# Different start addresses for the seven slots of the sequence batches

## The chip, the cores and the metric

The kernel runs on one core of one Trainium2 chip. The metric is the device time of one execution in microseconds (us). Before the change it is 725.52 us, the median of three runs (725.23 to 725.96).

## The reference, cut to what matters

```python
x = A_x                                             # 2048 x 576, float32
g = sigmoid((x * gate_w).sum(-1, keepdims=True))
a = linear_attention(x, A_wqkv, A_wo)               # 32 heads of 18
b = fourier(x)
out = g * a + (1 - g) * b

def fourier(x):
    a = einsum("bsd,ed->bse", x, dft_hid_re)        # 576 x 576
    b = einsum("bsd,ed->bse", x, dft_hid_im)
    return einsum("ts,bse->bte", dft_seq_re, a) - einsum("ts,bse->bte", dft_seq_im, b)
```

The change lies in the last line of `fourier`: two products of a 2048 x 2048 matrix with a 2048 x 576 matrix. The rest of the program (attention, and the products with the hidden-dimension matrices) are computed as before.

## The kernel before

**Precision.** TensorE multiplies in fp32r. Each float32 operand is split into a high part (ScalarE rounds a copy, helper `hi_of`, line 175) and a low part (VectorE subtracts, `lo_of`, line 185). A product takes three matmuls: high x low, high x high, low x high.

**Stages.** The keys and their features come first (lines 532 and 205), then the sums of keys and values (line 696), the queries and the output projection (line 205 again). Then come two pairs of stages: `Hidden.run` (line 979) makes the product of x with the real hidden matrix and leaves it on the chip as seven right-hand sides per pair of row blocks, after a scheme of the Strassen kind with seven products in place of eight. `sequence` (line 1133) multiplies the real sequence matrix with them. After that the same two stages run for the imaginary parts. The order of PE, ScalarE, VectorE and SyncE instructions is written out by hand.

**The right-hand sides** ("factors", tiles `fh` and `fl`) lie at `T_AT + p * TPAIR` for p = 0 to 7, seven rows of high and seven of low parts, each row 288 elements or 1152 bytes. `TPAIR` is 16128 bytes.

**The batches.** `sequence` runs over 32 batches: 8 row groups j by 4 batches b. One batch is 7 forms of 2 blocks of 128 x 128 of the sequence matrix, 7168 bytes in each partition (the constant `SLOT`). `Matrix.load` fetches four of the seven forms from HBM by one DMA of 512 KB on SyncE's queue (line 1070). `Matrix.make` forms the other three with VectorE (line 195), rounds all seven into a second tile, the high part (ScalarE, line 175), and subtracts in place, which leaves the low part (VectorE, line 185). In each of the 32 steps of `sequence` batch n + 3 is loaded, batch n + 2 is made, and batch n is multiplied: 7 products x 2 blocks x 3 matmuls = 42 matmuls, each with its own weight load of 128 x 128 from the batch and 288 columns of a factor.

**Where batches lie.** Seven slots of 7168 bytes lie one behind the other from `SLOT_AT`. Slots 3, 1, 4, 6 take the raw and later the low part of batch 1, 2, 3, 4 and so on in turn. Slots 2, 5, 0 take the high parts in turn. So twelve batches pass before a pair of slots comes again. Batch 0 lies elsewhere (`self.first`). 512 bytes lie between the end of the seventh slot and `Y_AT`; no batch uses them.

**What else uses this space.** `Hidden.run` keeps left-hand tiles (`xs`, `rests`) and weights (`w`) in the slots before batches need them. In the second `Hidden.run` (`swap` is 1) three groups of weights, `w(4)` to `w(6)`, lie from the start of slot 5 on, 4608 bytes each. They are loaded from HBM in the last steps of the first `sequence` (steps 28 and 29).

Of the kernel before, what the change touches and what calls it, by code (L numbers as in the profile page):

```python
# [20 lines left out]
HALF = D // 2  # L21
# [32 lines left out]
class Ring:  # L54


    def __init__(self, start, size, n):
        self.at, self.n = [start + i * size for i in range(n)], 0
# [11 lines left out]
SLOT_AT, SLOT = ACC_AT + NT * D * 4 + 256, 7 * BS * P * 4  # L70
# [21 lines left out]
class Layout:  # L92
# [5 lines left out]
    def __init__(self, swap):  # L98
        self.swap = swap
        slot = [SLOT_AT + k * SLOT for k in range(7)]  # L100
        self.low, self.high = [slot[k] for k in (3, 1, 4, 6)], [slot[k] for k in (2, 5, 0)]
        pair = [T_AT + p * TPAIR for p in range(NP)]
        self.first = pair[6], pair[7]
        self.xs = pair[1:6] if swap else [slot[0], slot[2], pair[4], pair[7], pair[5]]
        self.xs += [slot[0], slot[2], slot[0]]
        far, near = WF_AT + 4 * WF, slot[4]
        self.sums = pair[7] + SLOT + XR
        if swap:
            self.rests = [far, MIX_AT, pair[6] + SLOT, pair[6] + SLOT + XR, near, far,
                          pair[7] + SLOT, MIX_AT]  # L110
        else:
            self.rests = [near, MIX_AT, T_AT + 60416, MIX_AT + XR, far, near, MIX_AT, MIX_AT + XR]
# [10 lines left out]
    def w(self, k):  # L123
        if not self.swap:
            k = (0, 1, 2, 4, 5, 6, 3)[k]
        elif k > 3:
            return (SLOT_AT + 5 * SLOT + (6 - k) * 4 * HALF * 4,
                    (CONST_AT + 3584, CONST_AT + 3584 + HALF * 4, WF_AT + 4 * WF + XR)[k - 4])
        o = WF_AT + k * WF if k < 4 else SLOT_AT + 14 * XF + XR + (6 - k) * WF
        return o, o + 4 * HALF * 4  # L130
# [3 lines left out]
def kernel(  # L134
# [804 lines left out]
    class Hidden:  # L939
# [34 lines left out]
        def product(self, ps, p, k, start):  # L974
            x, (w, wl) = self.x[p, k], self.w[k]
            ops = [(x[:, a, c * P:c * P + P], w[:, 2 * c + b]) for c in range(2) for a, b in TURN]
            ops.append((self.rest[p][:96, 6 - k], wl[:96]))
            for n, (a, b) in enumerate(ops):
                nc.tensor.matmul(ps, a, b, start=(start and n == 0), stop=(n == len(ops) - 1),  # L979
                                 skip_group_check=True)  # L980
# [297 lines left out]
def _layouts(inputs):  # L1278
# [27 lines left out]
    def right(w):  # L1306

        main, rest = halves(w)
        quarters = ((0, 0), (1, 0), (1, 1), (0, 1))
        cols = (slice(0, HALF), slice(HALF, D))  # L1310
        main = np.stack([main[d][:, :, cols[c]] for d, c in quarters], axis=2)
        rest = np.stack([rest[d][:, cols[c]] for d, c in quarters], axis=1)
        return main, np.concatenate([rest] * 3)
# [42 lines left out]
```

## Time and profile before

| | |
|---|---|
| Median of the runs | 725.52 us |
| The profiled execution, its own time | 725.31 us |
| Its span, first to last instruction | 723.6 us |
| TensorE clock granted | 1.000 |
| PE busy | 718.9 us (99%) |
| VectorE (DVE) busy | 594.6 us (82%) |
| ScalarE (ACT) busy | 331.8 us (46%) |
| Line 1133 on the chain that ended last | 49% |

PE busy is the time in which a matmul was in flight; matmuls overlap, so PE is busy even where it runs below its best pace. The pace is better read as the number of matmuls that start in a stretch. The chain of work that ended last is followed back from the last instruction; its pieces, listed in order of time, show the stages one behind the other. A view of windows gives the busy time of each engine in chosen stretches. "Mean ns of one" of a matmul (about 294) is from its start to the modelled end of its results, more than twice the distance between two starts.

### The profile page before, as it was taken

The numbers are of one execution on the slowest core, as the hardware profiler recorded it, in microseconds if no ns is written. First come the engines' busy times: TensorE is split into PE (matmuls) and PEld (weight loads), VectorE is DVE, ScalarE is ACT, GpSimd is POOL, SyncE is SP. The second block draws the span as 40 slices with busy tenths as digits, with TensorE's granted clock in tenths as the row PEclk, the third lists the DMA queues.
The fourth block names the chain that finished last, engine by engine and source line by source line (L and its number), as shares of the span: only waits on it lengthen the run. The fifth ranks groups of instructions, "written<-read, shape, count | busy, mean of one in ns | idle before, by whom it ended". The sixth has DMA issues, their size and how long they took to land.

```text
span 723.6 us, 13786 instructions
## 1 busy us (share of the span) xinstructions
PE 718.9 (99%) x5436; PEld 718.3 (99%) x5436; DVE 594.6 (82%) x954; ACT 331.8 (46%) x519; POOL 54.1 (7%) x94
## 2 busy tenths in 40 slices
PE   9999999999999999999999999999999999999998
PEld 9999999999999999999999999999999999999997
DVE  5699876787999828989999999857889988778884
ACT  5998445678644534453434334223535432342331
POOL 1112200050131100000010000000000000000000
PEclk9999999999999999999999999999999999999999
DMA  7388887874594699544475586889963543454440
GB/s 256 105 286 297 305 304 214 295 223 118 182 358 177 228 321 388 160 153 131 157 249 189 167 289 198 287 313 401 380 214 130 175 143 136 125 179 153 153 154 34
DMA packets 54836, 157.83 MB, mean 218 GB/s; under 512 B 6388, under 2 KB 12084, under 8 KB 53748
## 3 DMA queue, kind: packets, MB, share of 16 engines
q1 hardware_dynamic: 45716, 118.44, 48.5%
q0 software_dynamic: 8768, 38.12, 14.5%
q8 instruction: 43, 0.70, 0.4%
q10 hardware_dynamic: 288, 0.39, 0.2%
q14 instruction: 21, 0.17, 0.1%
HBM read 114.06 MB, written 41.39 MB: 215 GB/s over the span
## 4 chain that ended last, share of the span: by engine, by line
PE 93%; DVE 6%; issue 0%; ACT 0%; DVEq 0%; POOL 0%; POOLq 0%
PE bank L1133 49%; PE bank L205 18%; PE bank L979 14%; PE bank L696 8%; PE bank L532 2%; DVE qs L185 1%; DVE acc L775 1%; DVE pz L767 1%; DVE den L768 1%; PE bank L231 1%; PE bank L678 0%; DVE xb L185 0%; DVE den L772 0%; PE bank L797 0%; DVE xb L195 0%
## 5 line engine op out<-in xcount | busy, mean ns | idle before, releaser
L1133 PE MATMUL bank<-fh,c 128*128 128x288 f32 x1792 | 354.7, 294 | 0.0
L1133 PEld LDWEIGHTS bank<-fh,c 128*128 128x128 f32 x1792 | 286.7, 188 | 0.0
L1133 PE MATMUL bank<-fl,c 128*128 128x288 f32 x896 | 263.6, 294 | 0.0
L175 ACT ACTIVATE c<-craw 128x1792 fp32r<-128x1792 f32 (+1 forms) x84 | 121.3, 1447 | 169.9 <-DVE craw L195 161.2
L1133 PEld LDWEIGHTS bank<-fl,c 128*128 128x128 f32 x896 | 168.7, 188 | 0.0
L185 DVE TENSOR_TENSOR c<-craw,c 128x1792 fp32r<-128x1792 f32 (+4 forms) x86 | 141.9, 1653 | 1.5 <-ACT c L175 1.4
L195 DVE TENSOR_TENSOR craw<-craw 128x256 f32<-128x256 f32 (+1 forms) x192 | 97.9, 512 | 22.0 <-DMA craw<-in_ci_dram 13.6
L205 PE MATMUL bank<-wd,xs 128*128 128x288 f32 (+1 forms) x784 | 105.9, 295 | 0.0
L205 PEld LDWEIGHTS bank<-wd,xs 128*128 128x128 f32 x784 | 104.6, 188 | 0.0
L979 PE MATMUL bank<-wf,xf 128*128 128x288 f32 x588 | 91.1, 295 | 0.0
L979 PEld LDWEIGHTS bank<-wf,xf 128*128 128x128 f32 x588 | 83.4, 189 | 0.0
L205 PE MATMUL bank<-mw,qs 128*128 128x288 f32 x448 | 61.8, 296 | 0.1
L696 PE MATMUL bank<-pk,c 128*128 128x288 f32 x448 | 60.6, 296 | 0.0
L205 PEld LDWEIGHTS bank<-mw,qs 128*128 128x128 f32 x448 | 59.8, 188 | 0.5 <-DVE qs L185 0.4
L696 PEld LDWEIGHTS bank<-pk,c 128*128 128x128 f32 x448 | 59.7, 189 | 0.0
L370 DVE SCALAR_TENSOR_TENSOR acc<-bank,e 128x288 f32<-128x288 f32 x64 | 28.5, 452 | 17.3 <-ACT e L369 17.1
L195 DVE TENSOR_TENSOR ys<-bank,ys 128x288 f32<-128x288 f32 x63 | 28.8, 456 | 16.0 <-PE bank L1133 12.6
L185 DVE TENSOR_TENSOR fl<-fl,fh 128x864 fp32r<-128x864 f32 (+1 forms) x32 | 34.5, 1093 | 6.6 <-ACT fh L175 5.3
L175 ACT ACTIVATE fh<-fl 128x864 fp32r<-128x864 f32 (+1 forms) x32 | 29.8, 950 | 16.6 <-DVE fl L195 16.6
L195 DVE TENSOR_TENSOR fl<-bank,y 128x288 f32<-128x288 f32 x48 | 21.6, 450 | 15.8 <-PE bank L979 15.8
L979 PE MATMUL bank<-wf,xr 96*128 96x288 f32 x112 | 33.3, 298 | 0.0
L195 DVE TENSOR_TENSOR ys<-ys,bank 128x288 f32<-128x288 f32 x47 | 21.2, 450 | 12.4 <-PE bank L1133 11.8
(106 smaller groups left out, 639.6 us busy)
## 6 DMA issues: line engine op xcount, KB each, us to landing
xf<-xm SPq DMA_DIRECT2D x42, 512.0 KB, 8.4
craw<-in_cr_dram SPq DMA_DIRECT2D x32, 512.0 KB, 3.6
craw<-in_ci_dram SPq DMA_DIRECT2D x32, 512.0 KB, 3.7
xm<-xb POOLq DMA_DIRECT2D x8, 1024.0 KB, 5.8
wf<-wm SPq DMA_DIRECT2D x14, 576.0 KB, 6.2
xraw<-in_xa_dram SPq DMA_DIRECT2D x25, 320.0 KB, 3.5
xr<-xr SPq DMA_DIRECT2D x14, 448.0 KB, 8.0
xm<-xb POOLq DMA_DIRECT2D x8, 768.0 KB, 7.4
```

What stands on the lines that cost most here:

```text
L175: return nc.scalar.activation(dst, src, AF.Copy, bias=bias)
L185: nc.vector.tensor_tensor(out=dst, in0=src, in1=hi, op=ALU.subtract)
L195: nc.vector.tensor_tensor(out=dst, in0=a, in1=b, op=op)
L205: nc.tensor.matmul(ps, a, b, start=(n == 0), stop=(n == len(pairs) - 1))
L231: nc.tensor.matmul(warm[:, :P], ones_f, ones_f, start=True, stop=True)
L370: nc.vector.scalar_tensor_tensor(dst, ps, 0.0, e, op0=ALU.max, op1=ALU.add)
L532: nc.tensor.matmul(ps[i][h], x[:, i_x * P:(i_x + 1) * P], wkt.row(h, j), start=(c == 0 and n == 0), stop=(c == KC and n == 1))
L696: nc.tensor.matmul(ps[h][:, :HALF], t[:, a, k], pk[s][:, b, half(h)], start=(s == 0 and n == 0), stop=(s == NT - 1 and n == len(passes) - 1))
L767: nc.vector.scalar_tensor_tensor(pz, acc[2 * k + i], EPS, zb, op0=ALU.add, op1=ALU.mult)
L768: nc.vector.tensor_reduce(out=d[:, i], in_=pz.rearrange("p (h d) -> p h d", d=DH), op=ALU.add, axis=AX.X)
L979: nc.tensor.matmul(ps, a, b, start=(start and n == 0), stop=(n == len(ops) - 1), skip_group_check=True)
L1133: nc.tensor.matmul(ps[q], c[x][:, l, k], factors[p](y, f), start=(p == 0 and i == 0), stop=(p == NP - 1 and i == 2))
```

## The change

The start of each slot's tile moves by an offset that is a multiple of 64 bytes. In the order in which they take turns, the slots for low parts move by 256, 64, 384 and 448 bytes, those for high parts by 64, 384 and 0. Modulo 256 bytes the low parts then start at 0, 64, 128, 192, and the high parts at 64, 128, 0. Before, all start at 0 (all of this relative to a base that all tiles share). No two slots overlap, and the last one stays inside the 512 bytes ahead of `Y_AT`. Weights `w(4)` to `w(6)` of the second `Hidden.run` move by 384 bytes, with slot 5. No instruction is added, removed or moved in its order.

```diff
     def __init__(self, swap):
         self.swap = swap
         slot = [SLOT_AT + k * SLOT for k in range(7)]
-        self.low, self.high = [slot[k] for k in (3, 1, 4, 6)], [slot[k] for k in (2, 5, 0)]
+        self.low = [slot[k] + o for k, o in ((3, 256), (1, 64), (4, 384), (6, 448))]
+        self.high = [slot[k] + o for k, o in ((2, 64), (5, 384), (0, 0))]
...
         elif k > 3:
-            return (SLOT_AT + 5 * SLOT + (6 - k) * 4 * HALF * 4,
+            return (SLOT_AT + 5 * SLOT + 384 + (6 - k) * 4 * HALF * 4,
                     (CONST_AT + 3584, CONST_AT + 3584 + HALF * 4, WF_AT + 4 * WF + XR)[k - 4])
```

## The prediction

> **What bounds the kernel now.** I read the page first, then what PE waits for, then the chain in order of time, then the pace of PE in single batches.
>
> ```profile
> span 723.6 us, 13786 instructions
> PE 718.9 (99%) x5436; PEld 718.3 (99%) x5436; DVE 594.6 (82%) x954; ACT 331.8 (46%) x519; POOL 54.1 (7%) x94
> ```
>
> The whole list of what PE waits for has one entry:
>
> ```profile
> engine line waited for: us in total, times, longest us
> PE bank L231 <- POOL ones_f L224: 1.1, 1, 1.1
> ```
>
> So once the warm-up has begun, PE is never recorded as idle for somebody else. The change can shorten the time only if PE's own matmuls follow each other faster; it can lengthen it by a slower pace, or by making somebody so late that a wait appears. The chain in order of time gives the pace of each large stage (start us, us, what):
>
> ```profile
> 20.42 44.59 PE bank L205 x336
> ...
> 85.16 12.85 PE bank L696 x96
> ...
> 261.68 51.98 PE bank L979 x392
> 313.66 177.16 PE bank L1133 x1344
> 490.82 52.07 PE bank L979 x392
> ```
>
> All these matmuls are 128 x 128 by 288 columns. The pieces divided by their counts: 132.7 ns from one matmul to the next in line 205 (44.59 / 336), 133.9 in line 696, 132.6 and 132.8 in line 979, 131.8 in line 1133. The stage that the change touches, line 1133, is already the fastest.
>
> Windows over `sequence`, cut where a batch's first matmul starts: batches 1, 2 and 3 of the first one, then batches 5 to 29 of each.
>
> ```profile
> core 0: us, PE busy (x) PEld busy (x) DVE busy (x) ACT busy (x) POOL busy (x), PEclk, DMA share, GB/s
> 319.08:324.66 5.58, 5.58 (x45) 5.58 (x43) 5.21 (x6) 5.58 (x5) 0.00 (x0) 1.00 0.10 41
> 324.66:330.19 5.53, 5.53 (x44) 5.53 (x43) 5.47 (x6) 1.31 (x2) 0.00 (x0) 1.00 0.27 98
> 330.19:335.73 5.54, 5.54 (x45) 5.54 (x44) 4.97 (x8) 3.59 (x3) 0.00 (x0) 1.00 0.32 95
> 341.26:479.59 138.33, 138.33 (x1052) 138.33 (x1051) 126.82 (x174) 49.92 (x34) 6.42 (x9) 1.00 0.66 220
> 570.52:708.85 138.33, 138.33 (x1052) 138.33 (x1051) 115.72 (x157) 44.62 (x31) 0.00 (x0) 1.00 0.45 148
> ```
>
> A batch is 42 matmuls, 25 batches are 1050 (the few more in the row were in flight at the edges). Both long windows take 138.33 us, 131.74 ns a matmul, although VectorE is busy 126.8 us in one and 115.7 in the other, and the DMA share is 0.66 and 0.45. Batches 2 and 3 lie in different slots, with ScalarE busy 1.31 and 3.59 us, and take 5.53 and 5.54 us. PE's pace thus doesn't feel VectorE, ScalarE or DMA, and not which slot is read: there is no conflict between engines here that spread slots could relieve. The clock is 1.00 throughout.
>
> What the pace may feel is where PE's own two operands lie. Line 1133 in detail (ns, min/median/max):
>
> ```profile
> L1133 PEld LDWEIGHTS bank<-fh,c x1792: 187/188/193, 313.4 to 719.7; 128*128 128x128 f32 x200
> L1133 PE MATMUL bank<-fh,c x1792: 288/295/302, 313.5 to 719.8; 128*128 128x288 f32 x200
> L1133 PEld LDWEIGHTS bank<-fl,c x896: 187/188/192, 313.5 to 719.4; 128*128 128x128 f32 x180
> L1133 PE MATMUL bank<-fl,c x896: 288/294/310, 313.6 to 719.5; 128*128 128x288 f32 x180
> ```
>
> Matmuls of one shape, at one clock, with no wait, last 288 to 310 ns, and weight loads 187 to 193. Something holds single ones up by a few ns, and the two windows of exactly equal length say that it does so in the same way each time. The likeliest source is the weight load of the next matmul, which runs while the columns of this one stream, both out of the same memory. The trace doesn't show the mechanism; this is my reading.
>
> **The change, part by part.** *The addresses.* A slot is 7168 bytes, 28 x 256, and a block 512 bytes, so before the change all weights of batches start at 0 modulo 256. The rows of the right sides are 1152 bytes, 4.5 x 256, so they start at 0 or 128. Weights and right sides meet in two relations only. After it the weights start at 0, 64, 128 or 192 in the low parts and 0, 64 or 128 in the high ones, and the mixture changes from batch to batch, through twelve pairs. Batch 0 lies elsewhere and stays as it is.
>
> The matmuls concerned: batches 1 to 31 of two sequences, 62 x 42 = 2604. Batch 1 already runs at 5.58 us / 42 = 132.9 ns with the same addresses modulo 256 as batch 2, so the pace has two values at the same places, depending on what went before. I price the 60 batches from 2 on, 2520 matmuls, at 131.74 ns now.
>
> The price of the new relations is not in the trace: nearly all operands of the program start at multiples of 128. Bounds from the nearest rows: slow side line 696, 133.9 ns, so 2520 x 2.1 ns = +5.4 us. Fast side the briefest matmul against the median, 288 against 295: 2520 x -7 ns = -17.6 us if every matmul became the briefest, a far end. The value that I take is that of line 979, 104.05 us / 784 = 132.7 ns: same shape, same order of three matmuls, same right sides of 1152-byte rows, but weights out of many tiles, as here after the change. The steady 131.74 ns is a pattern that repeats with every batch; a mixture that changes from batch to batch should lose it and fall to what the other stages and batch 1 have. 2520 x (132.7 - 131.74) = **+2.4 us**.
>
> Here the Trainium skill speaks against any effect. "TensorE: Matmul & The Clock Gate", section "Step-by-step: what each phase is for", says that TensorE reads its columns and its next weights through two independent ports and that loading the next weights takes nothing from the running matmul. By that rule the addresses wouldn't matter, and the sum would be 0. The same page's "Back-to-back issue gap" gives 288 / 2.4 + 2.5 = 122.5 ns for an isolated stream, an estimate; this case's 131.74 lies above it, so the trace doesn't fully bear the rule out.
>
> *ScalarE and VectorE.* They read and write the moved tiles. The nearest rows are a feature buffer that turns through three places 1184 bytes apart, 0, 160 and 64 modulo 256, and the batch's own operations:
>
> ```profile
> L369 ACT ACTIVATE e<-e x64: 443/445/447, 19.0 to 195.7; 128x288 f32<-128x288 f32 x64
> L370 DVE SCALAR_TENSOR_TENSOR acc<-bank,e x64: 444/451/459, 19.5 to 198.2; 128x288 f32<-128x288 f32 x64
> L185 DVE TENSOR_TENSOR c<-craw,c 128x1792 fp32r<-128x1792 f32 x62 | 125.0, 2019 | 1.5 <-ACT c L175 1.4
> ```
>
> 443 to 447 and 444 to 459 ns at all three places: no price, 0 us. If VectorE did become slower, its cover is the 8% in which it is idle in the first long window (126.82 of 138.33).
>
> *Loads.* A batch's load writes 4096 bytes a partition, now starting up to 192 past a multiple of 256. Its rows:
>
> ```profile
>   DMA craw<-in_ci_dram: 13.6, 10
> ...
> DMA to landing us min/median/max: 3.4/3.8/9.2
> ```
>
> VectorE already waits 13.6 us in all for these loads, and PE feels none of it, since a batch is made two batches (11 us) before its product. One more small transfer per partition is a few per cent of 3.8 us, 0 on the path. The Trainium skill, "DMA: Bandwidth & Descriptors", section "How a descriptor splits into AXI transactions", says that a descriptor off a 256-byte boundary costs an extra, partly unused transaction: 17 in place of 16, an estimate of 6% or 0.2 us per load; no row here shows it, and it would stay hidden.
>
> *Waits.* No instruction moves, so SyncE's and POOL's queues keep their order. Tiles now reach up to 384 bytes into the next slot of the old grid. What lay there in the stages of line 979 (rests in slot 4, forms of x in slots 2 and 3, weights in slots 5 and 6) was read at least one product group before the batch's load or rounding is issued, or was already waited for. The three groups of right sides move with slot 5, so that `w(6)` begins where slot 4 now ends and still overlaps slot 5 alone. Price 0; were it wrong, a load would stand in SyncE's queue for at most one product group and still have two batches in hand.
>
> **The sum.** The profiled execution took 725.31 us, 1.7 more than its span and 0.2 less than the median of 725.52. 725.31 + 2.4 = 727.7 there; at the median, **727.9 us**. A measurement of this kernel can tell about 0.2% from no change, 1.45 us, which is 0.58 ns a matmul.
>
> **The rivals.**
>
> *Faster: the new relations part the two streams.* If the hold-ups come from weights and columns reaching the same piece of memory together, starts 64 bytes apart may keep them apart. For it: 288 ns shows that matmuls with less hold-up exist. Against it: the relations 0 and 128 give almost the same paces in five stages, and two streams of different lengths slide past each other whatever their start. It counts from 0.58 ns below 131.74. Its price I take as a fifth of the way to the briefest matmul, 1.4 ns: 2520 x 1.4 = -3.5 us, 722.0.
>
> *Nothing: PE's pace doesn't depend on these addresses*, or the mixture averages to the same: 725.5. For it: paces from 131.7 to 132.9 are close together. Against it: 288 to 310 ns in one group. This is also the case in which the change doesn't do what it says. The Trainium skill's rule on the two ports ("TensorE: Matmul & The Clock Gate", above) would give this case too.
>
> *VectorE becomes the bound.* If operations with two inputs at different starts took a tenth longer, VectorE's 126.82 us over 25 batches would become 139.5 against PE's 138.33: 60 / 25 x 1.2 = +2.8 us, 728.3. It decides from +9%. Against it: the 444 to 459 ns above.
>
> **How the numbers follow.** My forecast, a slower pace: 0.42. Faster: 0.33; I have no row for starts of 64 and 192, so I can't push this lower. Nothing: 0.22. VectorE: 0.03. So faster 0.33, same 0.22, slower 0.45. The forecast's own range is 727.0 to 730.9, from 0.58 to 2.1 ns. As cases of both signs hold most of the chance, the range reaches from 721.0, somewhat beyond the faster case, to 730.0; outside lie the far end of the faster case and the slow end at line 696's pace.
>
> **What would show it.** Right: batches 5 to 29 take about 139.3 us in each sequence in place of 138.33 (1050 x 0.96 ns more), with batch lengths that differ and repeat after twelve; PE's waits stay a list of one; line 185 stays at 2019 ns; lines 205, 696 and 979 stay as they are. Wrong: both windows again 138.33 (addresses don't matter), windows below 137.7 (streams parted), or a wait of PE for VectorE or a DMA in `sequence` (a step above overlooked it).

## The result, and the profile after

The changed kernel takes **726.49 us** (median of 10 runs, 726.14 to 727.29) against 725.23 (10 runs of the kernel before beside it, 724.58 to 725.96): ratio 1.002, 95% interval 1.0012 to 1.0029. It is slower by 1.26 us; 2.4 us slower was forecast, and the measured value lies in the stated range. Lines of `kernel.py` are one further on in the profile after (1134 for 1133, 980 for 979, 186 for 185).

The page of the kernel after, its span and busy times:

```profile
span 724.9 us, 13787 instructions
PE 720.1 (99%) x5436; PEld 719.5 (99%) x5436; DVE 594.7 (82%) x954; ACT 331.7 (46%) x519; POOL 54.2 (7%) x94
```

The whole list of what PE waits for, after, is again the warm-up alone:

```profile
engine line waited for: us in total, times, longest us
PE bank L232 <- POOL ones_f L225: 1.1, 1, 1.1
```

The chain after, in order of time (start us, us, what):

```profile
20.12 44.59 PE bank L206 x336
...
261.39 52.00 PE bank L980 x392
313.39 177.86 PE bank L1134 x1344
491.25 52.20 PE bank L980 x392
543.45 174.73 PE bank L1134 x1320
```

Each line against the kernel before: 44.59 is unchanged, 51.98 became 52.00, 177.16 became 177.86, 52.07 became 52.20 and 174.03 became 174.73. The two sequences took 0.70 us more each. The second stage of line 980, in which the three groups `w(4)` to `w(6)` moved (they stream there as right sides), took 0.13 more. The chain reached line 206 at 20.12 in place of 20.42: that is the start of an execution, which the runs below also show to vary. 1.40 + 0.13 + 0.02 - 0.30 = 1.25, which is the difference of 1.3 us between the spans within rounding.

Windows of the kernel after, one for each of batches 1, 8, 9, 13, 20, 21 and 25 of the first sequence:

```profile
core 0: us, PE busy (x) PEld busy (x) DVE busy (x) ACT busy (x) POOL busy (x), PEclk, DMA share, GB/s
318.81:324.35 5.54, 5.54 (x45) 5.54 (x43) 5.17 (x6) 5.54 (x5) 0.00 (x0) 1.00 0.09 35
357.70:363.29 5.59, 5.59 (x45) 5.59 (x44) 5.42 (x9) 1.71 (x1) 0.00 (x0) 1.00 0.59 202
363.29:368.85 5.56, 5.56 (x44) 5.56 (x43) 5.49 (x7) 1.71 (x1) 0.00 (x0) 1.00 0.61 200
...
385.52:391.04 5.52, 5.52 (x44) 5.52 (x43) 5.38 (x10) 1.71 (x1) 0.00 (x0) 1.00 0.64 204
424.40:429.98 5.58, 5.58 (x45) 5.58 (x43) 5.41 (x9) 1.71 (x1) 0.00 (x0) 1.00 0.92 277
429.98:435.54 5.56, 5.56 (x44) 5.56 (x43) 5.42 (x10) 1.78 (x2) 0.00 (x0) 1.00 0.66 202
...
452.22:457.74 5.52, 5.52 (x45) 5.52 (x44) 4.94 (x7) 1.71 (x1) 0.00 (x0) 1.00 0.98 319
```

The lengths of batches now differ and come again after twelve: batches 8 and 20 take 5.58 to 5.59 us, 9 and 21 take 5.56, 13 and 25 take 5.52 although the DMA share is 0.64 in one and 0.98 in the other. A pair (low, high) gives the starts of the two parts modulo 256 bytes. Batch 9 is the pair (0, 0), the very place of the kernel before, where each batch from 2 on took 5.53; batch 13 is (0, 64). Batch 1 fell from 5.58 to 5.54.

VectorE's and ScalarE's work on the moved tiles, and the loads, in the view of the tile `craw` after:

```profile
L186 DVE TENSOR_TENSOR c<-craw,c x86: 417/2018/2028, 63.2 to 708.3; 128x1792 fp32r<-128x1792 f32 x62, 128x512 fp32r<-128x512 f32 x16, 128x256 fp32r<-128x256 f32 x4, 128x1024 fp32r<-128x1024 f32 x2
...
  DMA craw<-in_ci_dram: 14.8, 11
...
DMA to landing us min/median/max: 3.4/3.8/9.4
```

The median of 2018 ns is that of before, the loads still take 3.8 us, VectorE's waits for the loads of the second matrix are 14.8 us in place of 13.6, and PE waits for none of it. The loss lies in PE's pace alone.

### The profile page after: what moved, and what is told of

Read it like the earlier page. It is cut to its first block, busy times and chain, and to the rows that moved or that the text cites. A ratio compares the mean times of both kernels' runs of the same rounds, so it can differ in the third digit from the quotient of the medians.

```text
span 724.9 us, 13787 instructions
## 1 busy us (share of the span) xinstructions
PE 720.1 (99%) x5436; PEld 719.5 (99%) x5436; DVE 594.7 (82%) x954; ACT 331.7 (46%) x519; POOL 54.2 (7%) x94
## 4 chain that ended last, share of the span: by engine, by line
PE 93%; DVE 6%; issue 0%; ACT 0%; DVEq 0%; POOL 0%; POOLq 0%
PE bank L1134 49%; PE bank L206 18%; PE bank L980 14%; PE bank L697 8%; PE bank L533 2%; DVE qs L186 1%; DVE acc L776 1%; DVE pz L768 1%; DVE den L769 1%; PE bank L232 1%; PE bank L679 0%; DVE xb L186 0%; DVE den L773 0%; PE bank L798 0%; DVE xb L196 0%
## 5 line engine op out<-in xcount | busy, mean ns | idle before, releaser
L196 DVE TENSOR_TENSOR craw<-craw 128x256 f32<-128x256 f32 (+1 forms) x192 | 98.0, 512 | 23.0 <-DMA craw<-in_ci_dram 14.8
```

The lines of the kernel that those rows point to most:

```text
L196: nc.vector.tensor_tensor(out=dst, in0=a, in1=b, op=op)
```

## The experiments

The profile gives the length of a stretch of batches to 0.01 us, and it comes out the same in both sequences, so each place was run once, (0, 64) twice; only the changed kernel and the last one were timed repeatedly. The measure is 24 batches, 5 to 28, which are two turns of twelve. First the two kernels (before, then after), first and second sequence, line 1133 or 1134 on PE alone:

```profile
core 0: us, PE busy (x), PEclk, DMA share, GB/s
341.26:474.06 132.80, 132.80 (x1011) 1.00 0.66 219
570.52:703.32 132.80, 132.80 (x1011) 1.00 0.46 149
```

```profile
341.01:474.40 133.39, 133.39 (x1010) 1.00 0.65 218
571.10:704.49 133.39, 133.39 (x1011) 1.00 0.46 149
```

That is 5.533 and 5.558 us a batch.

**One place for all slots.** Theory: the mixture costs, because the relation changes with every batch. Rival: the places themselves cost. Kernels `all64`, and with 128 or 192 for each 64 `all128` and `all192`:

```diff
-        self.low, self.high = [slot[k] for k in (3, 1, 4, 6)], [slot[k] for k in (2, 5, 0)]
+        self.low = [slot[k] + o for k, o in ((3, 64), (1, 64), (4, 64), (6, 64))]
+        self.high = [slot[k] + o for k, o in ((2, 64), (5, 64), (0, 64))]
...
-            return (SLOT_AT + 5 * SLOT + (6 - k) * 4 * HALF * 4,
+            return (SLOT_AT + 5 * SLOT + 64 + (6 - k) * 4 * HALF * 4,
```

and `l0_h64`, with offsets that leave low parts at 0 and put high parts at 64 modulo 256:

```diff
-Y_AT = SLOT_AT + 7 * SLOT + 512
+Y_AT = SLOT_AT + 7 * SLOT + 1024
...
-        self.low, self.high = [slot[k] for k in (3, 1, 4, 6)], [slot[k] for k in (2, 5, 0)]
+        self.low = [slot[k] + o for k, o in ((3, 512), (1, 256), (4, 512), (6, 768))]
+        self.high = [slot[k] + o for k, o in ((2, 320), (5, 576), (0, 64))]
...
-            return (SLOT_AT + 5 * SLOT + (6 - k) * 4 * HALF * 4,
+            return (SLOT_AT + 5 * SLOT + 576 + (6 - k) * 4 * HALF * 4,
```

> All seven slots (and the three groups of right sides beside slot 5) 64 bytes further on: weights of every batch from 1 on start at 64 modulo 256, the right sides at 0 or 128 as before; the relation no longer changes from batch to batch. Mixture theory (what cost the time is that the relation changes with every batch, so that PE keeps falling out of its repeating pattern): all batches of a sequence after the first few take the same time again, near 5.53 us, and the time is 725.2, give or take 1. Place theory (a start 64 past a multiple of 128 costs by itself): equal batches too, but at 5.56 to 5.57 us, about +2 us in all, 727.

> All seven slots 128 bytes further on: the relations 0 and 128 between weights and right sides change places, nothing else. Mixture theory: equal batches near 5.53 us, 725.2 give or take 1. Place theory: the same two relations as before the change, so 5.53 us and 725.2 too. If the batches differ among themselves, both are wrong.

> All seven slots 192 bytes further on. Mixture theory: equal batches near 5.53 us, 725.2 give or take 1. Place theory: as for 64 bytes, 5.56 to 5.57 us and about 727.

> Low parts all at 0 modulo 256, high parts all at 64, by larger offsets (256 to 768 bytes, the area behind the slots 512 bytes further on). In the changed kernel the batches with this pair (1, 13, 25) were the briefest, 5.52 us against 5.53 before. Mixture theory: equal batches; where the pattern settles isn't known, between 5.50 and 5.56 us. Place theory: 5.52 us in every batch, 0.9 us less than before in all, 724.3.

24 batches of each sequence, `all64`:

```profile
341.00:474.52 133.52, 133.52 (x1010) 1.00 0.63 217
571.23:704.75 133.52, 133.52 (x1010) 1.00 0.45 148
```

`all128`:

```profile
340.88:474.96 134.08, 134.08 (x1011) 1.00 0.63 216
571.86:705.93 134.07, 134.07 (x1010) 1.00 0.45 148
```

`all192`:

```profile
341.59:475.27 133.68, 133.68 (x1011) 1.00 0.63 217
571.93:705.61 133.68, 133.68 (x1010) 1.00 0.45 148
```

`l0_h64`:

```profile
340.98:473.46 132.48, 132.48 (x1011) 1.00 0.65 219
569.88:702.37 132.49, 132.49 (x1011) 1.00 0.46 150
```

5.563, 5.587, 5.570 and 5.520 us a batch; the single times were 726.84, 728.05, 727.69 and 724.30 beside 725.02. The mixture theory falls: three kernels in which nothing is mixed are slower than the changed one. (`l0_h64` alone doesn't decide: both theories allowed 5.52.) The place theory holds for 64, 192 and (0, 64), but its claim for 128 falls too: weights at 128 meet right sides at 0 and 128 just as before, and yet a batch takes 0.054 us more. So the set of relations doesn't give the pace; that it matters which product meets which relation is the likely reading, and no run here tests it by itself.

**The other eight pairs of the change, one in each sequence.** Kernels `pairs_a` to `pairs_d` give each sequence one fixed pair, by offsets that depend on `swap`; the area behind the slots is 512 bytes further on, and `w(4)` to `w(6)` move by 768 bytes, 0 modulo 256. For `pairs_a`:

```diff
-        self.low, self.high = [slot[k] for k in (3, 1, 4, 6)], [slot[k] for k in (2, 5, 0)]
+        move = (0, 64, 256, 320, 320, 512, 576) if swap else (128, 256, 384, 512, 512, 640, 768)
+        self.low = [slot[k] + move[k] for k in (3, 1, 4, 6)]
+        self.high = [slot[k] + move[k] for k in (2, 5, 0)]
```

> One fixed pair of starts (low, high) modulo 256 in each sequence: (0, 128) in the first, (64, 0) in the second; the area behind the slots 512 bytes further on, as in the next three. The runs with one start for all slots showed that a fixed place has a steady pace of its own: 5.533 us a batch at (0, 0), 5.563 at (64, 64), 5.587 at (128, 128), 5.520 at (0, 64). Pair theory (the changed kernel's batches each run near the steady pace of their own pair, and its loss is the mean of twelve such paces): 5.55 in the first sequence and 5.57 in the second, as its batches 5 and 6 took, each within 0.02. Mixture theory (part of the loss comes from changing pairs): both below those, 5.53 to 5.54.

> (64, 128) in the first sequence, (128, 0) in the second. Pair theory: 5.55 and 5.56 us a batch, as batches 2 and 3 of the changed kernel, within 0.02. Mixture theory: 5.53 to 5.54 in both.

> (128, 64) in the first sequence, (192, 0) in the second. Pair theory: 5.565 and 5.54 us a batch, as batches 7 and 12 of the changed kernel, within 0.02. Mixture theory: 5.53 to 5.54 and 5.52.

> (192, 64) in the first sequence, (192, 128) in the second. Pair theory: 5.555 and 5.58 us a batch, as batches 4 and 8 of the changed kernel, within 0.02. Mixture theory: 5.53 and 5.56. With these all twelve pairs are known singly; on the pair theory the mean of the eight pairs of these four kernels is 5.562 (so that the mean of twelve is the 5.558 of the changed kernel), on the mixture theory under 5.55.

`pairs_a`, (0, 128) and (64, 0):

```profile
340.66:474.42 133.76, 133.76 (x1010) 1.00 0.64 217
571.68:705.60 133.92, 133.92 (x1010) 1.00 0.45 148
```

`pairs_b`, (64, 128) and (128, 0):

```profile
341.75:475.35 133.60, 133.60 (x1011) 1.00 0.65 217
572.03:705.79 133.76, 133.76 (x1011) 1.00 0.46 148
```

`pairs_c`, (128, 64) and (192, 0):

```profile
341.82:475.74 133.92, 133.92 (x1011) 1.00 0.64 217
572.39:705.91 133.52, 133.52 (x1011) 1.00 0.46 148
```

`pairs_d`, (192, 64) and (192, 128):

```profile
341.71:475.15 133.44, 133.44 (x1010) 1.00 0.65 218
571.86:705.94 134.08, 134.08 (x1010) 1.00 0.46 148
```

A batch takes 5.573, 5.580, 5.567, 5.573, 5.580, 5.563, 5.560 and 5.587 us; the single times were 727.70, 727.88, 727.97 and 728.06 beside 725.70. All eight are slower than (0, 0). The mixture theory, which had expected 5.52 to 5.56, is out. The pair theory holds in kind, each fixed pair having its own pace, within 0.03 us of its batch in the changed kernel, though beyond the expected 0.02 for (0, 128) and (192, 0). The mean of these eight is 5.573, over the expected 5.562. With (0, 0) 5.533, (64, 64) 5.563, (128, 128) 5.587 and (0, 64) 5.520 the mean of all twelve is 5.566. The changed kernel runs at 5.558. So going from pair to pair costs nothing on balance; it even gives 0.008 us a batch back. Single batches differ: (0, 0) loses by it, 5.56 in the changed kernel against 5.533.

In `pairs_a` PE waited once in `sequence`, outside the 24 batches; its list of waits has a second entry:

```profile
PE bank L1135 <- DVE c L187: 0.3, 1, 0.3
```

No other kernel here has a wait of PE for a batch. The trace leads back to one load: that of batch 29 was issued at 457.94 us and kept VectorE waiting for 3.45 us, until 464.89 (in the kernel before, 1.67 us, until 461.94), and the low part of batch 29 was then ready 0.29 us after PE wanted it. Why this load landed late is open.

**Everything moved together.** `arena64`:

```diff
-T_AT = 0
+T_AT = 64
```

> The kernel before with its whole memory area 64 bytes further on (T_AT is 64): every operand of every engine starts 64 bytes later, so all starts relative to each other stay. Relation theory (only where weights and right sides lie to each other modulo 256 counts): the same paces as before, 5.533 us a batch and 725.5 in all, give or take 0.3. Theory of absolute places (a start at 0 modulo 256 is itself what made the kernel before fast): batches near 5.56, as with 64 bytes for the batches alone, and about 727.

```profile
340.45:473.25 132.80, 132.80 (x1011) 1.00 0.64 218
569.70:702.50 132.80, 132.80 (x1010) 1.00 0.46 149
```

The chain of `arena64`:

```profile
19.63 44.59 PE bank L205 x336
...
260.88 51.97 PE bank L979 x392
312.85 177.16 PE bank L1133 x1344
490.01 52.07 PE bank L979 x392
542.08 174.03 PE bank L1133 x1320
```

These are the lengths of before to 0.01 us, in all these stages. A shift of 64 bytes costs when the batches alone make it (`all64`), and nothing when everything makes it: where operands lie to each other counts, not their absolute place. The time was 724.54 beside 725.08. This chain reached line 205 at 19.63 us, that of the profiled execution before at 20.42: what differs lies in the first 20 us. They vary from one execution to the next even of one kernel: batch 5 of `l0_h64` starts at 340.98 us above and at 340.57 when the same kernel is run again below. So single times within a microsecond decide nothing here, and windows do.

**Finer and other starts.** `pairs_e` and `pairs_f` put other pairs into the two sequences by the same edit as `pairs_a`.

> Low parts at 0 and high parts at 192 modulo 256 in the first sequence; low parts at 0, high parts at 32 in the second. The thirteen pairs measured so far have steady paces from 5.520 to 5.587 us a batch with no order that a theory gives, so (0, 192) is expected between these ends, near their mean of 5.566. If only the 64-byte line of a start counts, 32 bytes act as 0 does and the second sequence takes 5.533 a batch; if the start counts more finely, something else comes out.

> A look for a place that beats (0, 64): (low, high) at (32, 64) in the first sequence, (0, 96) in the second. (0, 32) and (0, 64) took 5.520 us a batch, (0, 0) 5.533, (0, 128) 5.573. If the pace follows the 64-byte line, rounded up, in which the high part starts, 96 acts as 128: 5.573 for the second sequence; and (32, 64) acts as (64, 64): 5.563. If only low parts at exactly 0 are favourable, the first sequence is slower than 5.54 in any case. Anything under 5.52 would be a better place.

`pairs_e`, (0, 192) and (0, 32):

```profile
341.63:475.39 133.76, 133.76 (x1011) 1.00 0.65 217
571.93:704.41 132.48, 132.48 (x1011) 1.00 0.46 150
```

`pairs_f`, (32, 64) and (0, 96):

```profile
340.72:473.68 132.96, 132.96 (x1011) 1.00 0.65 218
570.31:704.23 133.92, 133.92 (x1011) 1.00 0.46 148
```

5.573, 5.520, 5.540 and 5.580 us a batch (726.34 beside 725.08, 726.35 beside 724.98). With low parts at 0, 32 acts for the high parts as 64 does, not as 0, and 96 acts nearly as 128. For the low parts 32 doesn't act as 64: (32, 64) takes 5.540 and (64, 64) 5.563. It lies just at the limit of 5.54 that was set for it, and so leaves open whether only low parts at 0 are favourable. Starts that differ by 32 bytes can differ in pace. Nothing came out below 5.520.

**The better version, timed.** `l0_h64` again:

> The kernel with low parts at 0 and high parts at 64 in both sequences again, timed in rounds against the kernel before. Its batches took 5.520 us against 5.533, 0.0133 less, and batch 1 0.045 less: 2 x (30 x 0.0133 + 0.045) = 0.9 us less, a ratio of 0.9988. The pair theory has nothing else change; if the interval lies at 1 or above, something outside the two sequences gave the gain back.

723.90 us (11 runs, 723.59 to 724.92) against 725.16 (14 runs, 724.53 to 726.06): ratio 0.9984, interval 0.9975 to 0.9993. It is faster than the kernel before by 1.26 us (0.9 was expected), between 0.5 and 1.8 by the interval. Of this, 0.8 us lies in the large stages: each sequence takes 0.44 less, the second stage of line 980 0.09 more. The rest is within the interval. The changed kernel's 726.49 is slower still, though the two were not timed side by side. The windows are those of the first run:

```profile
340.57:473.05 132.48, 132.48 (x1010) 1.00 0.64 219
569.48:701.96 132.48, 132.48 (x1011) 1.00 0.46 150
```

## Why the prediction was right, and where it was not

*What bounds the kernel.* Right. PE waits for no other engine in `sequence` before or after, and the two sequences with different DMA shares keep equal lengths to 0.01 us in every kernel that has the same places in both.

*No conflict between engines to relieve.* Right: VectorE's 2018 ns and the loads' 3.8 us did not move with the tiles, and fixed places give equal lengths in two sequences in which VectorE and the DMA engines are busy to different degrees.

*ScalarE, VectorE, loads, waits at 0.* Right. The load's price, if there is one, stayed hidden. The extra transaction that the Trainium skill's "DMA: Bandwidth & Descriptors", section "How a descriptor splits into AXI transactions", speaks of can be neither seen nor ruled out here: the median landing is 3.8 us before and after, but two executions of `l0_h64` give 3.7 and 3.9, as far apart as the estimate of 0.2 us.

*The price of the new relations*, 0.96 ns a matmul: right in sign, too large. Batches 2 to 31 take 5.558 in place of 5.533 us, which is 0.59 ns a matmul (24 batches in 133.39 us; the forecast's 0.96 ns would be 133.77). The sign that was to show it, 139.3 us for batches 5 to 29, came out at 138.94 in both sequences. 60 x 0.025 = 1.5 us, less 0.04 us for each of the two batches 1, which I had left unchanged: 1.4 in place of the forecast 2.4. The step that failed is taking line 979's pace as the value. A mixture of twelve places runs near the mean of their own paces, 5.566; line 979's 132.7 ns would be 5.573. Nor was line 979 the same shape throughout, as I read it. From the list of forms before:

```profile
L979 PE MATMUL bank<-wf,xf 128*128 128x288 f32 x588 | 91.1, 295 | 0.0
...
L979 PE MATMUL bank<-wf,xr 96*128 96x288 f32 x112 | 33.3, 298 | 0.0
```

One matmul in seven works on 96 rows in place of 128. By the starts in that trace, a start comes 134.8 ns after such a matmul, and 132.4 ns after one of 128 rows. With 132.4 in place of 132.7 the sum would have been +1.7 us. That this is nearer to the 1.4 measured is no proof that line 979 is the right row for a mixture. The 0.13 us of the second stage of line 980 was priced at nothing: I took the move of `w(4)` to `w(6)` as a question of waits alone. A slip besides: 2520 x 2.1 ns is 5.3 us, not 5.4, so the forecast's own range ends at 730.8.

*The reason that I gave for it*, a repeating pattern that a mixture loses: wrong. Fixed places repeat just as well and take 5.520 to 5.587. The kernel before wasn't fast because it was steady, but because (0, 0) is a good place: of the fourteen pairs with multiples of 64 that had a fixed run here (the twelve of the change, (192, 192) and (0, 192)), it is the second fastest after (0, 64). Spreading the starts replaced a good place by average ones. So the direction came out as forecast for a reason that doesn't hold, and that part was luck: from a slower start than (0, 0), say (128, 128) at 5.587, the same spreading to 5.558 would be a gain. The stated range, 721.0 to 730.0, held the main rivals' times too.

*The rival "faster by parting the streams".* It didn't come about for the mixture, but two places, (0, 64) and (0, 32), are faster: 0.32 ns a matmul, well short of the 1.4 ns that I gave it. Whether they part two streams isn't shown.

*The rival "nothing".* Out by the interval. The Trainium skill's rule behind it, the two independent ports in "TensorE: Matmul & The Clock Gate", section "Step-by-step: what each phase is for", gives no reason for places to differ. Here 24 batches take 132.48 to 134.08 us by place alone, so what I drew from that rule, no effect at all, is off by up to 1.2%. Whether the two reads meet each other no run shows.

*The rival "VectorE becomes the bound".* Out: PE doesn't wait for it.

What stays open is the mechanism. Shown is that PE's pace depends on where the weights lie relative to what stays in place, low and high parts each counting, and not on the absolute place. That what counts there is the rows of the right sides is inferred from PE reading nothing else in `sequence`, and from the lengths not feeling how busy the other engines are; the second stage of line 980, where right sides moved and weights stayed, bears it out (see the last section). That it is the next weight load and the streaming columns that get into each other's way is argued, not shown: no experiment took one of the two reads away. Nor do I have a rule that gives the pace of a pair: (0, 0) takes 5.56 in the changed kernel (batches 9 and 21) and 5.533 alone, so the neighbouring batches count as well.

## What to carry to other kernels

Where matmuls follow each other without a wait, a change of addresses can act on TensorE's own pace, as here, and its size is read from windows cut at equal counts of matmuls, not from the total, whose start varies by nearly as much. Spreading buffers over different starts against a supposed conflict gave about the mean of all places here; if one fixed place is already better than that mean, spreading loses. It is cheap to try fixed places, one in each of two like stages, and to keep the best: here that was 0.16% in the time, 0.11% by the large stages alone.

## What the runs showed of the hardware that I had not expected

Two places 32 bytes apart, (0, 64) and (0, 96), differ by 1.1% in the pace of the same matmuls (24 batches in 132.48 and 133.92 us), and the same place gives the same length to 0.01 us in both sequences, in another execution (`l0_h64` twice) and with everything moved by 64 bytes.

The other operand counts too. In the second stage of line 980 the three moved groups are the streaming side, while the weights stayed. The stage takes 52.07 to 52.09 us where the groups start at 0 modulo 256 (before, `arena64`, all `pairs` kernels), 52.16 at 64 (`all64`, `l0_h64` twice), 52.20 at 128 (the changed kernel, `all128`) and 52.10 at 192 (`all192`).

The fixed places' 24 batches are not spread evenly: 132.48, 132.80, 132.96, 133.44, 133.52, 133.60, 133.68, 133.76, 133.92, 134.08 are all whole multiples of 0.08 us, most of them of 0.16. So a batch, or two of them together, lasts a whole multiple of 6.67 ns. In some kernels two successive batches differ and their sum repeats: in `all64` they take 5.558 and 5.568 in turn, by the starts of their first matmuls. No run here shows what sets the step.
